# A linear-attention and mixture-of-experts kernel: two v casts moved to ScalarE, a third exp buffer, the first expert products split, and a planner that knows a shared memory port

## The chip, the cores and the metric

The kernel runs on one core of one Trainium2 chip. The metric is the device time in microseconds of one execution. Before the change it was 982.22 us (median of 3 runs, 981.87 to 985.09). The span that a profile shows is about 1.8 us shorter than the time of the same execution.

Engine names: PE is TensorE's matmuls, PEld its weight loads, DVE is VectorE, ACT is ScalarE, POOL is GpSimd, SP is SyncE.

## The reference, cut to what matters

```python
def phi(x):                                     # elu + 1
    return np.where(x > 0, x, np.exp(x) - 1.0) + 1.0
q_p, k_p = phi(q), phi(k)                       # q, k, v: 8 batches, 8 heads, 576 x 64
kv  = np.einsum('bhsd,bhse->bhde', k_p, v)
z   = np.sum(k_p, axis=2)
x   = einsum(q_p, kv) / (einsum(q_p, z) + 1e-6)   # -> 4608 rows of 512
P   = exp(x @ w_gate - max);  8 rounds of row and column normalisation
out = sum over e of P[:, e] * (relu(x @ w1[e]) @ w2[e])    # 8 dense experts, F = 1024
```

The attention is small. The expert products are almost all of the work.

## The kernel before

The attention is done in 16 units, each a batch and half of its heads. A unit loads k, q and v, makes phi of k and q (exp on ACT, min and max on DVE), casts v to 16 bits on GpSimd, and sends them through kv, den, num and two transposes to x transposed (`xT`). The products of expert 0 run beside all this as far as their rows of `xT` are complete. Matmuls of nothing (`warm`) fill PE until then.

The program emits its instructions through a planner. It simulates the engines with estimated times and emits each task when its simulated turn comes. Each engine then runs its own list in that order, on the chip as well:

```python
def add(self, eng, fn, deps=(), prio=0.0, acq=(), use=(), lat=0.0, after=0.0): ...
def slot(t):
    r = t["ready"]
    ...                                    # and when buffers of its pools come free
```

The parts of a unit that the change touches (cut):

```python
def att(b, g):
    n = 2 * b + g
    ...
        (nc.gpsimd if n in (2, 3) else nc.sync).dma_start(...)   # k, q, v of the unit
    ...
    te = fadd(("act", 1.17), f_e, ...)                           # exp
    tph[nm] = fadd(("dve", 1.35), f_m, deps=[te, tt_], ...)      # min, max: phi
    ...
    def f_v(e):
        copy(e, gvv["tile"][:, :, :, 0:D], gin["v"]["tile"])     # the v cast
    tvv.append(fadd(("pool", 1.3), f_v, deps=[ta, tin["v"]], ...))
    vcast[n] = tvv[0]
```

The order of the first weights is set with the cast:

```python
att(0, 0)
att(0, 1)
w_t = {0: load_w1(0, prio=-290.0, parts=2, deps=[vcast[0]])}   # issued on GpSimd's queue
```

`deps` is known to the planner alone. It says that the load is planned after the cast. No data passes from the cast to the load, so no semaphore is made for it. The load waits on the chip only because both stand in GpSimd's one list.

The softmax here doesn't subtract the row's maximum and nothing guards it: scores larger than these inputs give would overflow.

## Time and profile before

| | before |
|---|---|
| time, median of 3 | 982.22 us |
| span of the profiled execution | 982.2 us |
| PE busy | 962.2 us, 98% |
| first kv product of unit 0 starts | 9.12 us |
| denominators of unit 0 reach DVE (`rden`, 1e-6 added, just before the reciprocal) | 14.74 us |
| first product of expert 0 starts | 22.53 us |
| PE idle from 22.5 to 120 us | 8.6 us |

### The profile page before, as it was taken

The numbers are of one execution on the slowest core, as the hardware profiler recorded it, in microseconds if no ns is written. First come the engines' busy times: TensorE is split into PE (matmuls) and PEld (weight loads), VectorE is DVE, ScalarE is ACT, GpSimd is POOL, SyncE is SP. The second block draws the span as 40 slices with busy tenths as digits, with TensorE's granted clock in tenths as the row PEclk, the third lists the DMA queues.
The fourth block names the chain that finished last, engine by engine and source line by source line (L and its number), as shares of the span: only waits on it lengthen the run. The fifth ranks groups of instructions, "written<-read, shape, count | busy, mean of one in ns | idle before, by whom it ended". The sixth has DMA issues, their size and how long they took to land.

```text
span 982.2 us, 21403 instructions
## 1 busy us (share of the span) xinstructions
PE 962.2 (98%) x8716; PEld 792.7 (81%) x8716; DVE 771.7 (79%) x1561; ACT 563.2 (57%) x1034; POOL 127.9 (13%) x171
## 2 busy tenths in 40 slices
PE   7899999999999999999999999999999999999997
PEld 4455564488888888888888888888888888888885
DVE  6898869967777777777777777777777777777774
ACT  4798754565555555555555555555555555555552
POOL 4111200001111111111111111111111111111110
PEclk9999999999999999999999999999999999999999
DMA  9886953162226312272225322272225322236663
GB/s 318 257 303 239 265 160 140 65 127 77 75 76 142 97 73 76 76 161 76 77 75 137 101 76 75 76 162 76 76 76 137 102 76 76 76 103 168 161 161 98
DMA packets 47029, 121.99 MB, mean 124 GB/s; under 512 B 4177, under 2 KB 18001, under 8 KB 46929
## 3 DMA queue, kind: packets, MB, share of 16 engines
q1 hardware_dynamic: 32128, 99.76, 30.3%
q0 software_dynamic: 14480, 20.33, 11.5%
q8 instruction: 68, 1.11, 0.5%
q10 hardware_dynamic: 320, 0.52, 0.1%
q14 instruction: 33, 0.26, 0.1%
HBM read 119.69 MB, written 17.69 MB: 140 GB/s over the span
## 4 chain that ended last, share of the span: by engine, by line
PE 89%; DVE 1%; ACT 1%; issue 0%
PE ye L809 33%; PE hq L627 23%; PE att L627 11%; PE Zye L627 6%; PE Zye L809 6%; PE ye L706 5%; PE hq L536 4%; PE xt_ps L387 0%; PE kv_ps L306 0%; PE num_ps L371 0%; PE lg_ps L405 0%; DVE tk L281 0%; PE qt_ps L332 0%; ACT tq L272 0%; PE den_ps L347 0%; ACT qpT L221 0%
## 5 line engine op out<-in xcount | busy, mean ns | idle before, releaser
L823 DVE SCALAR_TENSOR_TENSOR acc<-ye,P_sb,acc 128x256 f32<-128x256 f32 x620 | 264.9, 477 | 95.3 <-PE ye L809 77.9
L627 PEld LDWEIGHTS <-W 128*128 128x128 f16 x2016 | 197.1, 98 | 23.7
L809 PEld LDWEIGHTS <-S 128*128 128x128 f16 x1984 | 194.1, 98 | 22.7 <-issue 0.3
L809 PE MATMUL ye<-T,S 128*128 128x256 f16 x1488 | 192.8, 273 | 0.1
L833 POOL TENSOR_TENSOR acc<-acc,st 128x256 f32<-128x256 f32 x124 | 87.5, 725 | 625.6 <-ACT st L830 620.7
L653 ACT ACTIVATE h<-hq 128x512 f16<-128x512 f32 x126 | 76.3, 606 | 160.8 <-PE hq L627 160.8
L627 PEld LDWEIGHTS <-w 128*128 128x128 f16 x1512 | 147.6, 98 | 23.3 <-issue 1.0
L809 PEld LDWEIGHTS <-h 128*128 128x128 f16 x1488 | 145.6, 98 | 16.8
L627 PE MATMUL hq<-xs,W 128*128 128x256 f16 x1008 | 151.2, 273 | 0.0
L627 PE MATMUL att<-xs,W 128*128 128x256 f16 x1008 | 151.2, 272 | 0.0
L627 PE MATMUL hq<-xs,w 128*128 128x256 f16 x1008 | 140.7, 272 | 0.8 <-DVE h L656 0.8
L782 DVE TENSOR_TENSOR S<-h 128x1024 f16<-128x1024 f16 x124 | 85.4, 688 | 57.9 <-ACT h L653 57.9
L656 DVE CUSTOM_DVE_ANT_0 h<-att,s 128x512 f16<-128x512 f32 x126 | 86.7, 688 | 13.1 <-ACT s L643 13.1
L830 ACT ACTIVATE st<-Zye,P_sb 128x256 f32<-128x256 f32 x124 | 52.1, 471 | 78.0 <-PE Zye L809 78.0
L643 ACT COPY s<-hq 128x512 f32<-128x512 f32 x126 | 75.0, 595 | 36.7 <-PE hq L627 36.7
L650 ACT ACTIVATE h<-Zye 128x512 f16<-128x512 f32 x126 | 75.2, 597 | 35.1 <-PE Zye L627 35.1
L656 DVE CUSTOM_DVE_ANT_0 h<-hq,s 128x512 f16<-128x512 f32 x126 | 86.5, 686 | 0.8 <-PE hq L627 0.7
L639 ACT COPY Zye<-hq 128x512 f32<-128x512 f32 x126 | 73.3, 581 | 16.3 <-PE hq L627 16.3
L706 PE MATMUL ye<-w,h 128*128 128x512 f16 x320 | 77.6, 379 | 0.9 <-DVE acc L223 0.9
L627 PE MATMUL Zye<-xs,w 128*128 128x256 f16 x504 | 75.6, 273 | 0.0
L647 ACT COPY s<-att 128x512 f32<-128x512 f32 x126 | 74.5, 591 | 0.0
L536 PE MATMUL hq<-xT,w 128*128 128x512 f16 x288 | 70.6, 379 | 2.4 <-ACT h L540 2.2
(90 smaller groups left out, 963.1 us busy)
## 6 DMA issues: line engine op xcount, KB each, us to landing
xs<-xd SPq DMA_DIRECT2D x63, 896.0 KB, 4.6
w<-in_moe_w_dram POOLq DMA_DIRECT2D x14, 1024.0 KB, 11.7
out_dram<-acc SPq DMA_DIRECT2D x68, 128.0 KB, 2.4
kin<-in_k_dram SPq DMA_DIRECT2D x14, 576.0 KB, 6.0
qin<-in_q_dram SPq DMA_DIRECT2D x14, 576.0 KB, 5.0
vin<-in_v_dram SPq DMA_DIRECT2D x14, 576.0 KB, 6.4
xd<-xst SPq DMA_DIRECT2D x9, 512.0 KB, 2.6
xd<-xT SPq DMA_DIRECT2D x9, 256.0 KB, 7.1
```

Source lines behind the costliest of these rows:

```text
L536: nc.tensor.matmul(ghq["tile"], lhsT=gw1["tile"][:, c, ts(f, P)], rhs=xT[:, c, ds(512 * g, 512)], start=(c == 0), stop=(c == NDT - 1))
L627: nc.tensor.matmul(dst[:, p, :], lhsT=lhs(p, c), rhs=rhs(c), start=(first and p == 0 and c == 0), stop=(c == 1), skip_group_check=True)
L643: nc.scalar.copy(out=gs2["tile"], in_=gX["tile"])
L647: nc.scalar.copy(out=gs5["tile"], in_=gR["tile"])
L650: nc.scalar.activation(out=hd(0, 0), in_=Zt[1], func=AF.Relu)
L653: nc.scalar.activation(out=hd(1, 0), in_=gX["tile"], func=AF.Relu)
L656: nc.vector._custom_dve(TENSOR_ADD_SAT, out=dst, in0=ps, in1=sb, s0=3.0e38, s1=0.0)
L706: nc.tensor.matmul(gy[tt]["tile"], lhsT=gh["tile"][:, f, ds(P * tt, P)], rhs=gw2["tile"][:, f, :], start=(f == 0), stop=(f == NFT - 1))
L782: nc.vector.tensor_tensor(out=Sx[:, i], in0=a0, in1=a1, op=op)
L809: nc.tensor.matmul(bank(g_)[:, s, :], lhsT=lhs(s, kk), rhs=rhs(kk), start=(new and s == 0 and kk == 0), stop=(kk == 3), skip_group_check=True)
L823: nc.vector.scalar_tensor_tensor(out=dst(), in0=bank(g_)[:, s, :], scalar=P_sb[:, gg, e:e + 1], in1=dst(), op0=ALU.mult, op1=ALU.add)
L833: nc.gpsimd.tensor_tensor(out=dst(), in0=dst(), in1=gst["tile"], op=ALU.add)
```

## The change

Its intent, in the order of the diff: the planner is told that a v cast on GpSimd locks the memory port that DVE's phi needs; a third buffer for the results of exp; the v casts of units 0 and 1 on ACT, which is idle there; the first two tiles of the first expert product split in halves of the contraction, so that half can run on the `xT` of unit 0 alone.

```diff
     def run(self):
+        locked = [0.0]
         def slot(t):
-            r = t["ready"]
+            r = max(t["ready"], locked[0]) if t["port"] else t["ready"]
 ...
+            if t["lock"] and e == "pool":
+                locked[0] = t["done"]
 ...
-    p_e = S_.pool(2)
+    p_e = S_.pool(3)
 ...
+    VACT = (0, 1)
 ...
-            tph[nm] = fadd(("dve", 1.35), f_m, ..., prio=pr)
+            tph[nm] = fadd(("dve", 1.35), f_m, ..., prio=pr, port=True)
 ...
-        tvv.append(fadd(("pool", 1.3), f_v, ..., prio=pr))
+        tvv.append(fadd(("pool", 1.2) if n not in VACT else ("act", 1.17), f_v, ..., prio=pr, lock=True))
 ...
-        for f in range(NFT):
-            ghq = S_.grp(p_hq)
+        jobs = [(f, 0, NDT) for f in range(NFT)]
+        if g == 0:
+            jobs = [(f, c, c + 2) for c in (0, 2) for f in range(2)] + jobs[2:]
+        for f, c0, c1 in jobs:
 ...
-            t1 = add(("pe", 0.87), f_hq, deps=[tw1[f // 4], prev_hq[0]] + xd_, ...)
+            t1 = add(("pe", 0.2175 * (c1 - c0)), f_hq,
+                     deps=[tw1[f // 4], prev_hq[0]] + xd_[0:c1 if g == 0 else None], ...)
```

(cut: the signatures of `add`, `bufs=3` at the exp tile, and the bookkeeping of the halves.)

More of the change, by code (lines that the diff above doesn't have):

```diff
@@ L31, in grp, with add @@
         return {"pool": pool, "users": [], "tile": None}
-    def add(self, eng, fn, deps=(), prio=0.0, acq=(), use=(), lat=0.0, after=0.0):
+    def add(self, eng, fn, deps=(), prio=0.0, acq=(), use=(), lat=0.0, after=0.0, lock=False, port=False):
         if isinstance(eng, tuple):
@@ L37, in add @@
         k = len(self.t)
-        t = {"eng": eng, "fn": fn, "prio": prio, "acq": tuple(acq), "lat": lat, "kids": [], "nd": 0,
+        t = {"eng": eng, "fn": fn, "prio": prio, "acq": tuple(acq), "lat": lat, "lock": lock, "port": port, "kids": [], "nd": 0,
              "ready": after, "done": None, "id": k}
@@ L264, in f_e @@
             def f_e(_, ge=ge, nm=nm):
-                ge["tile"] = fp.tile([P, 2, NJ, D], FP16, tag="e", name="e" + nm)
+                ge["tile"] = fp.tile([P, 2, NJ, D], FP16, tag="e", name="e" + nm, bufs=3)
                 nc.scalar.activation(out=ge["tile"], in_=gin[nm]["tile"], func=AF.Exp)
@@ L285, in att @@
                        acq=[gt[nm]], use=[gin[nm]], prio=pr)
-            tph[nm] = fadd(("dve", 1.35), f_m, deps=[te, tt_], use=[ge, gt[nm], gin[nm]], prio=pr)
+            tph[nm] = fadd(("dve", 1.35), f_m, deps=[te, tt_], use=[ge, gt[nm], gin[nm]], prio=pr, port=True)
         gvv = S_.grp(p_vv)
@@ L294, in f_v @@
             copy(e, gvv["tile"][:, :, :, 0:D], gin["v"]["tile"])
-        tvv.append(fadd(("pool", 1.3), f_v, deps=[ta, tin["v"]],
-                        use=[gvv, gin["v"]], prio=pr))
+        tvv.append(fadd(("pool", 1.2) if n not in VACT else ("act", 1.17), f_v, deps=[ta, tin["v"]],
+                        use=[gvv, gin["v"]], prio=pr, lock=True))
         vcast[n] = tvv[0]
@@ L529, in layer1, with f_hq @@
         tha = add(("none", 0.0), f_ha, deps=[prev_hq[0]], acq=[gh], prio=g - 400.0)
-        for f in range(NFT):
-            ghq = S_.grp(p_hq)
-            def f_hq(_, f=f, ghq=ghq):
-                ghq["tile"] = hqp.tile([P, 512], FP32, tag="hq", name="hq")
-                for c in range(NDT):
+        ghqs = [S_.grp(p_hq) for f in range(NFT)]
+        jobs = [(f, 0, NDT) for f in range(NFT)]
+        if g == 0:
+            jobs = [(f, c, c + 2) for c in (0, 2) for f in range(2)] + jobs[2:]
+        for f, c0, c1 in jobs:
+            ghq = ghqs[f]
+            def f_hq(_, f=f, ghq=ghq, c0=c0, c1=c1):
+                if c0 == 0:
+                    ghq["tile"] = hqp.tile([P, 512], FP32, tag="hq", name="hq")
+                for c in range(c0, c1):
                     nc.tensor.matmul(ghq["tile"], lhsT=gw1["tile"][:, c, ts(f, P)], rhs=xT[:, c, ds(512 * g, 512)],
@@ L540, in f_rl @@
                 nc.scalar.activation(out=gh["tile"][:, f, :], in_=ghq["tile"], func=AF.Relu)
-            t1 = add(("pe", 0.87), f_hq, deps=[tw1[f // 4], prev_hq[0]] + xd_, acq=[ghq], use=[gw1],
+            t1 = add(("pe", 0.2175 * (c1 - c0)), f_hq, deps=[tw1[f // 4], prev_hq[0]] + xd_[0:c1 if g == 0 else None],
+                     acq=[ghq] if c0 == 0 else [], use=[gw1] + ([ghq] if c0 > 0 else []),
                      prio=g + 0.1 * f + 0.35)
@@ L544, in layer1 @@
             x_users.append(t1)
+            if c1 < NDT:
+                continue
             th.append(add(("act", 0.6), f_rl, deps=[t1, tha], use=[ghq, gh], prio=g - 400.0))
```

## The prediction

> **What bounds the kernel now.** I read the engine totals first, then the table of stretches, then the timeline of the first 40 us.
>
> ```profile
> PE 962.2 (98%) x8716; PEld 792.7 (81%) x8716; DVE 771.7 (79%) x1561; ACT 563.2 (57%) x1034; POOL 127.9 (13%) x171
> PE 89%; DVE 1%; ACT 1%; issue 0%
> ```
>
> The first line is the busy time of each engine, the second the share of each engine in the chain that ended last. TensorE (PE) sets the time. The table of stretches (columns: length, busy us and instructions of PE, PEld, DVE, ACT, POOL, then granted PE clock, DMA share, GB/s) says where it does not:
>
> ```profile
> 9.10:22.50 13.40, 11.48 (x131) 7.03 (x131) 11.71 (x25) 5.90 (x11) 9.17 (x12) 0.87 1.12 325
> 22.50:30.00 7.50, 4.41 (x44) 2.13 (x41) 5.17 (x9) 5.83 (x8) 2.73 (x2) 1.00 1.15 277
> 60.00:80.00 20.00, 17.59 (x174) 10.27 (x172) 19.45 (x36) 19.31 (x31) 3.96 (x4) 1.00 0.88 300
> 140.00:160.00 20.00, 20.00 (x117) 9.97 (x115) 17.79 (x48) 9.16 (x17) 0.00 (x0) 1.00 0.56 215
> 300.00:900.00 600.00, 599.92 (x5465) 534.10 (x5463) 471.74 (x919) 334.51 (x635) 76.34 (x106) 1.00 0.34 96
> ```
>
> From 120 us to 900 us PE is full. The total of matmuls is fixed by the algorithm and the change removes none, so time can only be won where PE waits or runs filler: before 22.5 us, and in the idle gaps from 22.5 to 120 us, which add up to 8.6 us (97.5 us less the PE busy time of those stretches: 3.1, 0.2, 1.4, 2.4, 0.25 and 1.2 us). "Busy" before 22.5 us includes 34 warm-up matmuls that compute nothing. The useful matmuls of the first two attention units are per unit kv 0.69, transposes of q 0.68, den 0.42, num 0.77, transposes of x 0.72 us = 3.3 us, so 6.6 us for both; about 16 of the first 22.5 us are a pure start-up latency. The 6.6 us of PE idle after 900 us is the drain at the end, and the change does not touch it.
>
> What the start-up consists of, from the timeline (start, length, engine, line, operation, count, idle before):
>
> ```profile
> 7.92 1.15 POOL L225 CAST vv<-vin 128x1152 f16<-128x1152 f32 x1 [6.61 <-DMA vin<-in_v_dram]
> 7.94 1.43 DVE L275 TENSOR_SCALAR eq<-eq 128x1152 f16<-128x1152 f16 x1
> 9.41 1.43 DVE L281 SCALAR_TENSOR_TENSOR tq<-qin,eq 128x576 f16<-128x576 f32 x2
> ...
> 12.39 1.15 POOL L225 CAST vv<-vin 128x1152 f16<-128x1152 f32 x1 [0.28 <-DMA vin<-in_v_dram]
> ...
> 12.41 2.40 DVE L281 SCALAR_TENSOR_TENSOR tk<-kin,ek 128x576 f16<-128x576 f32 x2
> ...
> 14.74 0.17 DVE L353 TENSOR_SCALAR rden<-den_ps 128x20 f32<-128x20 f32 x1
> ...
> 22.45 1.18 ACT L221 COPY xT<-xt_ps 128x576 f16<-128x576 f16 x2 [3.05 <-PE xt_ps L387]
> ...
> 22.53 0.99 PE L536 MATMUL hq<-xT,w 128*128 128x512 f16 x3
> ...
> 23.68 1.24 PE L536 MATMUL hq<-xT,w 128*128 128x512 f16 x5 [0.16 <-ACT xT L221]
> ```
>
> DVE's min on eq takes 1.43 us here; the same instruction on ek at 6.10 us took 0.46 us. The pair that makes tk at 12.41 us takes 2.40 us where the pair at 6.60 us took 1.43 us. Both lie beside a GpSimd cast of v. Each costs DVE 0.97 us on the chain input, exp, phi, transpose, den, reciprocal, normalise, x transposed, first expert product. In the whole front I find nine such lengthened instructions, 7.1 us in sum: these two, and seven (5.1 us) between 27 and 113 us.
>
> **What the Trainium skill says.** "SBUF — State Buffer", section "Who interferes with whom": GpSimd's port pair is DVE's second pair, an exclusive lock for a whole instruction; tensor_scalar in a two-port mode, or a DVE instruction with two SBUF inputs against a GpSimd instruction that reads SBUF, blocks or is blocked, and the one that issued first wins. The trace agrees: 1.15 us of cast, 0.97 us of delay, and where DVE was first the cast itself is the long one (1.58 us at 27.25 us against 1.15 us). The same section says ACT has ports of its own, so a cast there should delay nothing. "TensorE: Matmul & The Clock Gate", section "What's actually happening": a clock gate halves PE's clock after a stretch of low activity. The trace agrees: the granted clock is 0.5 from about 11.7 to 15.1 us. "Perfetto Trace Analysis", section "Identifying the Most-Contended Engine", prefers weight-load time and useful work to matmul busy time; I follow it by not counting warm-up as work.
>
> **The change part by part.**
>
> First, the v casts of units 0 and 1 go to ACT, after its exps. vin lands at 7.9 us; ACT ends the exp of q at 7.54 us, so the first cast ends near 9.1 us, as on GpSimd. The cost of 1.16 us (ACT's other f32 to f16 passes over 128x1152 take that) falls where ACT was idle from 7.54 to 9.46 us. DVE's eq then ends at 8.45, tq at 9.93 instead of 10.84 us. Next on DVE come four kvz copies (all four now on DVE, 0.93 us as at 29.35 us) and the shorter qpT copy, to about 11.3 us; min 0.46 and tk 1.43 us uncontended end at 13.1 instead of 14.8 us. So rden, and with it xn and x transposed of unit 0, come 1.7 us earlier. Unit 1: its v cast on ACT comes after exp and add of q, 13.4 to 14.6 us, a us later than on GpSimd, but its kv product sits behind unit 0's x transposes on PE, at 17.44 us before and near 15.75 us now, so that is hidden. Unit 1's x transposed should be complete about 1.7 us earlier, near 21.9 instead of 23.6 us.
>
> Second, the split. In the instruction order of the changed PE, two hq matmuls now stand in unit 1's wait for qpT, where three warm-ups stood, and the two halves of the second tile fill the wait for the last x copy. The kernel before already ran c=0 and 1 of the first tile ahead of that copy, as waits are per instruction (three matmuls at 22.53, the next at 23.68 us). So the split brings two matmuls, 2 x 0.217 = 0.43 us, not four. The first half of w1 was issued at 9.0 us and landed 5.9 us later, at 14.9 us, so the early pair does not stall PE's queue at about 17.3 us.
>
> Third, the third e buffer lets an exp start before the previous phi is finished. At the start it gives nothing: the second exp of k began at 9.46 us and its data lands at 2.26 + 7.1 = 9.4 us.
>
> Fourth, the planner now puts phi after a cast that is planned beside it. This only reorders: 14 casts stay on GpSimd. From 20 us on the orders of PE, ACT and DVE differ nearly everywhere until attention ends, then are the same. In the changed order PE has 160 instead of 136 second-layer matmuls behind it when the last x transpose comes, with 164 first-layer ones in both: 24 x 0.217 = 5.2 us more useful work. Part is a later end of attention (planned phis wait), part less PE waiting. I count 1 us as real: of the 5.1 us of later DVE delays perhaps half goes, and in 40 to 80 us, where DVE and ACT are over 93% busy and PE idles 3.9 us, perhaps 40% of that reaches PE.
>
> Against this stands DMA. Transfers run without a pause from 2 to 40 us at 207 to 408 GB/s, so vin of units 2 and 3 (landed 22.8 and 27.2 us) comes no earlier. PE has ready hq work then, so I take only 0.3 us off.
>
> Sum: 1.7 + 0.43 + 1.0 - 0.3 = 2.8 us; with a little for gaps behind the earlier relus, 3 us. 982.2 - 3.0 = 979.2.
>
> **Rivals.** (a) The inputs absorb the head start: unit 2 and 3 wait for DMA, and all but the 0.4 us of the split and a little hq work is lost, 981.3 us. For it: GpSimd waited 2.95 and 3.15 us for vin there. Against: PE idled 3.1 us in that stretch for ACT's relus (1.4 us) and for tq (1.6 us), not for DMA. (b) The new order fits the chip much better: all of the planned 5.2 us is real on top of the start-up, 975 us. For it: nine delays gone would be 7.1 us of DVE time in its fullest stretch. Against: PE idles only 4 us from 40 to 80 us, and nothing stops a real cast from colliding when real times slip from planned ones. (c) The order fits worse: a static order that takes hq groups ahead of kv makes PE wait in line and exps come late on ACT, giving back 2 to 3 us: 982 to 983 us. For it: ACT has two more passes, 2.3 us. Against: they lie before 15 us, where ACT has slack.
>
> **Range and chances.** (a) and (b) set the ends: 976.3 to 981.4 us. Two per cent is 19.6 us, more than all PE idle and start-up latency that a reorder could reach, so within 2%: 0.985; faster 0.01, slower 0.005.
>
> **What would show it.** Right: no GpSimd cast before 20 us; eq's min 0.46 us and unit 1's tk pair 1.43 us; rden near 13.1 us; first hq matmuls as a pair near 17.5 us; the steady run of hq near 20.8 us; PE full after 120 us as before. Wrong: PE idle between 22.5 and 120 us not below 8 us, DVE delays beside casts still near 5 us, or the half-clock stretch moved onto the first hq products. The prediction fails low if attention's end falls behind and PE runs dry, and high if those gaps vanish.

## More of the kernel before

The prediction shows the main lines. Two more views are needed later. The first is the timeline of GpSimd (start, length, engine, line, operation, count, idle before and its releaser):

```profile
9.00 1.66 POOL L207 DMA_DIRECT2D w<-in_moe_w_dram  x2
10.66 0.72 POOL L253 DMA_DIRECT2D kin<-in_k_dram  x1
...
22.95 1.15 POOL L225 CAST vv<-vin 128x1152 f16<-128x1152 f32 x1 [2.95 <-DMA vin<-in_v_dram]
```

The w1 load follows the first v cast at 9.00 us. The cast of unit 2 waits for its input until 22.95 us.

The second is the DMA view, for the stretch from 7 to 8 us (queue, packets, MB, share of the 16 engines' time) and for the first 13 us (transfer, count, size, median us from issue to landing):

```profile
q1 hardware_dynamic: 183, 0.40, 103.4%
...
vin<-in_v_dram SPq DMA_DIRECT2D x2, 576.0 KB, 7.6
```

Until w1 is issued, the hardware queue with the inputs of units 0 and 1 has the DMA engines to itself and moves 0.40 MB in a microsecond.

One caution on this profile. Its execution took 983.97 us, almost 2 us over the median of the kernel before.

## The result, and the profile after

| | before | after |
|---|---|---|
| median of the same rounds (4 runs each) | 982.29 us (981.87 to 985.09) | 985.08 us (984.15 to 986.27) |
| ratio | | 1.0023, 95% interval 1.0001 to 1.0045 |

A ratio here is the mean time of one kernel's runs over the mean of the other's runs of the same rounds, so it is not quite the ratio of the medians that are quoted. The class is "same", but the time is 2 to 3 us up, where 3 us down was predicted, and it is outside the predicted range.

The engine totals and the chain that ended last hardly differ from before. PE still sets the time:

```profile
PE 962.5 (98%) x8716; PEld 792.9 (81%) x8716; DVE 768.1 (78%) x1560; ACT 567.2 (58%) x1037; POOL 128.9 (13%) x169
PE 92%; DVE 4%; ACT 2%; DMA 2%; issue 1%; SPq 0%; DVEq 0%; ACTq 0%
```

The table of stretches answers to the one in the prediction:

```profile
9.10:22.50 13.40, 9.50 (x110) 5.98 (x110) 8.44 (x22) 7.82 (x10) 5.33 (x8) 0.87 1.10 338
22.50:30.00 7.50, 6.15 (x40) 2.84 (x38) 4.73 (x8) 5.04 (x8) 3.49 (x4) 1.00 1.13 294
60.00:80.00 20.00, 19.05 (x200) 11.52 (x200) 17.43 (x38) 16.68 (x26) 4.11 (x3) 1.00 0.56 189
300.00:900.00 600.00, 599.91 (x5466) 534.21 (x5464) 471.82 (x919) 334.60 (x635) 76.66 (x107) 1.00 0.34 96
```

The middle of the kernel is the same, and 60 to 80 us is fuller than before, 19.05 against 17.59 us. The loss is at the start. The timeline of the first 27 us, with the same instructions as those that the prediction shows of before:

```profile
1.44 1.66 POOL L211 DMA_DIRECT2D w<-in_moe_w_dram  x2
...
8.05 0.46 DVE L281 TENSOR_SCALAR eq<-eq 128x1152 f16<-128x1152 f16 x1
8.54 1.43 DVE L287 SCALAR_TENSOR_TENSOR tq<-qin,eq 128x576 f16<-128x576 f32 x2
...
10.09 1.16 ACT L225 CAST vv<-vin 128x1152 f16<-128x1152 f32 x1 [2.46 <-DMA vin<-in_v_dram]
...
14.72 1.43 DVE L287 SCALAR_TENSOR_TENSOR tk<-kin,ek 128x576 f16<-128x576 f32 x2
...
16.06 0.17 DVE L359 TENSOR_SCALAR rden<-den_ps 128x20 f32<-128x20 f32 x1
...
21.23 0.59 PE L547 MATMUL hq<-xT,w 128*128 128x512 f16 x2
...
25.03 0.99 PE L547 MATMUL hq<-xT,w 128*128 128x512 f16 x3
```

Read from the bottom: the steady run of expert products starts at 25.03 us (22.53 before), `rden` of unit 0 at 16.06 us (14.74 before), the v cast at 10.09 us (7.92 before), because its input came late. The two DVE delays are gone, as planned: min on eq takes 0.46 us and the pair for tk 1.43 us. The first line tells why the input came late. The w1 load went out at 1.44 us, 7.6 us earlier than before.

The DMA view of the same two stretches as before:

```profile
q1 hardware_dynamic: 88, 0.19, 56.2%
q0 software_dynamic: 90, 0.09, 54.9%
...
vin<-in_v_dram SPq DMA_DIRECT2D x2, 576.0 KB, 11.8
w<-in_moe_w_dram POOLq DMA_DIRECT2D x2, 512.0 KB, 14.2
```

From 7 to 8 us the inputs now share the DMA engines with w1, about half of the time each, and move 0.19 MB where they moved 0.40 MB. v takes 11.8 us to land, not 7.6 (median of units 0 and 1). The Trainium skill, "DMA: Bandwidth & Descriptors", section "SWDGE vs HWDGE vs iDMA", says that software-generated and hardware-generated transfers feed different internal queues of each DMA engine and that the engine serves them in turn. The trace agrees: w1 moves almost nothing before 6 us (a share of 4.8% from 5 to 6 us), when k and q of unit 0 have nearly landed, and then both queues move side by side, with shares of 56.2% and 54.9% from 7 to 8 us. The inputs that pay are v of unit 0 and all of unit 1, which were issued after w1.

### The profile page after: what moved, and what is told of

It is laid out like the page before. It is cut to its first block, busy times and chain, and to the rows that moved or that the text cites. A ratio compares the mean times of both kernels' runs of the same rounds, so it can differ in the third digit from the quotient of the medians.

```text
span 982.9 us, 21418 instructions
## 1 busy us (share of the span) xinstructions
PE 962.5 (98%) x8716; PEld 792.9 (81%) x8716; DVE 768.1 (78%) x1560; ACT 567.2 (58%) x1037; POOL 128.9 (13%) x169
## 4 chain that ended last, share of the span: by engine, by line
PE 92%; DVE 4%; ACT 2%; DMA 2%; issue 1%; SPq 0%; DVEq 0%; ACTq 0%
PE ye L823 33%; PE hq L641 23%; PE att L641 11%; PE ye L720 6%; PE Zye L641 6%; PE Zye L823 6%; PE hq L547 5%; DMA vin<-in_v_dram 2%; PE xt_ps L393 1%; PE num_ps L377 1%; PE kv_ps L312 1%; PE qt_ps L338 1%; DVE tk L287 1%; DVE tq L287 1%; DVE xn L382 1%
```

## The experiments

Every kernel below was compared with runs of the kernel before on the same chip in the same rounds. All gave the right result but for two that are wrong, as told there.

A measure used below, called **lead**: in the kernels that keep the plan of the kernel before, PE's list is the same, so the start of the same group of matmuls can be compared between two profiles. The lead is how many us earlier it starts than in the control (e12_before_again); a minus says later.

### Does the early w1 load cost the time?

**e1_gate.** The changed kernel with a tiny copy of one column of the cast v on GpSimd in front of the first w1 load. The load now has to wait as it did before. No order is planned anew.

```diff
+                if e == 0 and nm == "w1" and i == 0:
+                    gt_s = const.tile([P, 1], FP16, tag="gate", name="gate")
+                    nc.gpsimd.tensor_copy(out=gt_s, in_=vv_t[0][:, 0, 0, 0:1])
                 nc.gpsimd.dma_start(out=dst, in_=AP(...))
```

> The changed kernel, with one tiny GpSimd copy (128x1) that reads the first cast v put in front of the first weight load on GpSimd's queue, so that this load waits for the cast on ScalarE as it waited for the cast on GpSimd before. Instruction orders are else unchanged. Theory T (the change set the first weight load free: it is issued at 1.44 us instead of 9.0 us, takes bandwidth from the first q, k and v, and vin lands at 10.1 instead of 7.9 us; all else in the change is a gain): vin lands near 7.9 us, first kv product near 9.1 us, rden of unit 0 near 13.1 us instead of 16.1 us, and the time is 979 to 981 us, 4 to 6 us under the changed kernel and 1 to 3 us under the kernel before. Rival R1 (the new instruction orders from 22 to 120 us cost it): first kv is early too, but the time stays within 1.5 us of 985. Rival R2 (the casts delay ScalarE's exps): 983 to 985 us.

Measured: 982.38 us (981.22 to 983.22), before 981.95; ratio 1.0003 (0.9990 to 1.0016). The changed kernel itself was at 1.0022 in its repeat below. So the early load costs 0.0019 of 982 us, 1.9 us (the two intervals together leave some 1.8 us either way). The start is then nearly as predicted: v cast on ACT at 8.17, `rden` at 13.67, steady expert products at 21.47 us; 0.6 to 0.7 us are missing, with the kv and q transposes of unit 0 at a halved clock (1.02 and 1.14 us). Still nothing is gained on the kernel before. Theory T is half right: the load costs time, but what is left is not a gain of 1 to 3 us.

**e2_early_w1.** The other way round: the kernel before with both w1 loads issued at set-up, every other order kept.

```diff
+        early = e == 0 and nm == "w1"      # tile made and both dma_starts emitted at once;
+            if early: fn(None, now=True)   # the planned task then does nothing
```

> The kernel before, with only the two halves of the first weight load issued ahead of everything on GpSimd's queue; plan and orders of all else unchanged, casts of v on GpSimd, no split. Theory T: vin of unit 0 lands near 10 us instead of 7.9, the first kv product moves to about 11.3 us, and the time rises by 2 to 4 us over the kernel before (984 to 986 us). R1 and R2, which see no harm in the early load: within 1 us of the kernel before.

Measured: 987.20 us (984.97 to 988.87), before 981.95; ratio 1.0051 (1.0038 to 1.0065). The early load alone costs the kernel before 5 us: w1 goes out at 1.24 us, the v casts start at 10.20 and 20.46 us (7.92 and 12.39 before), `rden` of unit 0 at 16.16 us. That is more than the 2 to 4 us that theory T expected.

**e6_after_again.** The changed kernel once more, to have it beside the others.

```diff
 (no edit)
```

> The changed kernel itself once more, on the same chip as the next three runs, so that the cost of the early weight load can be read against them directly. All theories: 984 to 986 us; granted clock 0.995 to 0.997, below the 0.998 to 1.000 of the kernel before.

Measured: 984.94 us (983.34 to 985.76), before 982.17; ratio 1.0022 (1.0010 to 1.0035). The loss is real.

**e7_gate_warm.** e1_gate with eight more warm-ups before the first kv product, so that the half-clock stretch at the start (mean granted clock 0.87 from 9.1 to 22.5 us in the first profiles of both kernels) goes away.

```diff
+        nwarm[0] += 1
-        nc.tensor.matmul(yw[0], ...)
+        for _i in range(9 if nwarm[0] == 16 else 1):
+            nc.tensor.matmul(yw[0], ...)
```

> The changed kernel with the first weight load held back (as e1_gate) and eight more warm-up matmuls before the first kv product, which fill PE's gap from about 7.3 to 9.1 us. Theory H (what e1_gate failed to win of the predicted 3 us is eaten by half-clock stretches at the start: kv and q transposes of unit 0 took 1.02 and 1.14 us instead of 0.69 and 0.68): those two are back at 0.69 and 0.68 us, rden of unit 0 near 12.9 us, mean granted clock 0.999 or more, time 980.5 to 981.7, about 1 us under e1_gate. Rival (a head start at the front is lost downstream whatever its size, in order waits and DMA): first parts as above, time within 0.5 us of e1_gate's 982.4.

Measured: 982.94 us (981.36 to 986.11), before 982.17; ratio 1.0009 (0.9992 to 1.0027). The half clock at the start went (1.00 throughout), and no gain came: theory H fell. Two of the six runs are at 986 us, so this is shown only to about 1.7 us.

### The parts alone, each planned anew

**e3_casts_on_pool.** The changed kernel with all v casts on GpSimd.

```diff
-    VACT = (0, 1)
+    VACT = ()
```

> The changed kernel with all casts of v on GpSimd again (planner, third e buffer and split stay). GpSimd's cast holds the first weight load back again, so T: load issued near 9.0 us, vin at 7.9 us, the two DVE delays of 0.97 us at 7.9 and 12.4 us are back, and the time is 980.5 to 982.5 us, under the changed kernel by 2.5 to 4.5 us. R1 (orders from the planner cost it): 984 us or more. R2: 981 to 983 us as well; it is told from T by e1_gate and by the second run of this set.

Measured: 987.88 us (985.99 to 990.20), before 981.95; ratio 1.0057 (1.0043 to 1.0071). A miss for theory T: without the ACT casts, and with the w1 load nearly in its old place (9.57 us), it is slower still, as rival R1 said of the new orders.

**e5_act_casts_only.** The kernel before with the two casts on ACT alone, planned anew.

```diff
+    VACT = (0, 1)
-        tvv.append(fadd(("pool", 1.3), f_v, ...
+        tvv.append(fadd(("pool", 1.3) if n not in VACT else ("act", 1.17), f_v, ...
```

> The kernel before with only the first two casts of v on ScalarE, no gate, planner and split as before. T: the first weight load is issued near 1.4 us, first kv near 11.3 us, time 984 to 986 us as in the changed kernel: this part alone carries the loss. R1 (the planner's knowledge of the port costs it): within 1 us of the kernel before. R2: 983 to 985 us too, but with vin landing at 7.9 us.

Measured: 988.21 us (987.72 to 989.78), before 981.95; ratio 1.0064 (1.0052 to 1.0076). w1 goes out at 1.43 us as theory T said, but the loss is larger than its 984 to 986 us, so the new order costs something of its own.

**e4_act_casts_gate.** e5 with the gate of e1_gate.

```diff
 (e5_act_casts_only and the gate)
+                    nc.gpsimd.tensor_copy(out=gt_s, in_=vv_t[0][:, 0, 0, 0:1])
```

> The kernel before with only the first two casts of v on ScalarE and the first weight load held back by a tiny GpSimd copy; planner and split as before. It is e5_act_casts_only but for the gate. Theory T: the load near 10 us, vin near 8 us, first kv near 9.4 us, and the time falls by 4 us or more from e5's 988.2, to 981 to 984 us. If e5's loss came from its instruction orders after 40 us (half-clock stretches at 50 and 67 us in its profile), it stays at 986 us or more.

Measured: 990.27 us (989.69 to 990.96), before 982.17; ratio 1.0078 (1.0066 to 1.0091). A clear miss. The gate did not help here. In its trace PE waits 2.9 us for the w2 load between 30 and 40 us, and its clock is halved once near 52 us.

**e8_split_only.** The kernel before with the split of the first expert products.

```diff
+        if g == 0:
+            jobs = [(f, c, c + 2) for c in (0, 2) for f in range(2)] + jobs[2:]
```

> The kernel before with only the split of the first two products by halves of the contraction. By the prediction's count: 0.4 us less, 981.3 to 982 us. Rival S (any edit makes the planner draw a new order after 25 us, and orders differ by several us whatever the edit does itself): 984 us or more, with PE idle or half-clock stretches after 40 us that the kernel before has not.

Measured: 983.90 us (982.15 to 984.33), before 982.17; ratio 1.0011 (0.9998 to 1.0024). No gain, where 0.4 us was expected. The pair ran early, at 18.63 us, as meant.

**e10_port_only.** The kernel before with the planner's knowledge of the port, and the cast's estimate of 1.2 us.

```diff
+            r = max(t["ready"], locked[0]) if t["port"] else t["ready"]
+            if t["lock"] and e == "pool":
+                locked[0] = t["done"]
```

> The kernel before with only the planner's knowledge of the port (lock and port flags, cast at 1.2 instead of 1.3 in the plan); casts on GpSimd, two e buffers, no split. My prediction took 1 us of gain for this part (with the third e buffer): 980.7 to 981.7. Rival S (a new order is a new draw, and most draws are worse than the tuned one): 984 to 988 us, with PE waits or half-clock stretches after 40 us.

Measured: 983.58 us (982.05 to 985.21), before 981.92; ratio 1.0011 (0.9994 to 1.0027). No gain, where about 1 us was expected.

**e11_e3_only** and **e19_e3_again.** The third exp buffer alone, twice.

```diff
-    p_e = S_.pool(2)
+    p_e = S_.pool(3)
-                ge["tile"] = fp.tile([P, 2, NJ, D], FP16, tag="e", name="e" + nm)
+                ge["tile"] = fp.tile([P, 2, NJ, D], FP16, tag="e", name="e" + nm, bufs=3)
```

> The kernel before with only the third e buffer. Prediction: nothing at the start, so 981.5 to 982.5 us. Rival S: a new draw of the order, 983 to 988 us.

Measured: 981.05 us (980.65 to 981.57), before 981.92; ratio 0.9985 (0.9973 to 0.9997). Of all kernels here only this run's interval lies below 1. Because it was picked out of many, it was run again:

> The third e buffer alone once more: it was the only one of the kernels with an interval below 1 (0.9985, 0.9973 to 0.9997), picked out of many, so it could be luck of the run. If the gain is real: 0.998 to 0.999, below 981.3 us. If it was luck of the draw: 0.9995 to 1.0005.

Measured: 981.78 us (981.14 to 982.85), before 982.35; ratio 0.9994 (0.9981 to 1.0008). The two together suggest about 0.001, 1 us. It is the best kernel that was found, and its gain is not settled.

What these six edits teach is that the parts do not add up. An edit that makes the planner run with other times gives another order for all of the attention, and such orders differ by up to 0.8%. The next group therefore keeps the plan.

### The casts alone, with the plan kept

**e12_before_again.** The kernel before, as control.

```diff
 (no edit)
```

> The kernel before itself, for a second profile. Its first profile came from an execution 2 us slower than its median (983.97 against 982.2 us) and shows 8.6 us of PE idle between 22.5 and 120 us. If part of the predicted gain was counted from idle that a usual execution has not, the profile of a usual one (981 to 982.5 us) shows less: 6 to 7.5 us. If the idle is the same 8.6 us, the base of my sum was right and the loss is elsewhere.

Measured: 981.98 us (981.69 to 982.50), before 981.92; ratio 0.9995 (0.9982 to 1.0007). Its profile has 6.5 us of PE idle from 22.5 to 120 us, as expected of a usual execution.

**e13_cast_same_plan.** The planner still believes that the casts are on GpSimd. Only the emitted instruction goes to ACT. The order on PE, DVE and SP is that of before; ACT has two casts more, GpSimd two fewer and the gate.

```diff
-            copy(e, gvv["tile"][:, :, :, 0:D], gin["v"]["tile"])
+            copy("act" if n < 2 else e, gvv["tile"][:, :, :, 0:D], gin["v"]["tile"])
+                    nc.gpsimd.tensor_copy(out=gt_s, in_=vv_t[0][:, 0, 0, 0:1])
```

> The kernel before with its plan and every instruction order kept, only that the first two casts of v are emitted on ScalarE at their planned place instead of GpSimd, and the first weight load is held back by a tiny GpSimd copy of the first cast v. No new order is drawn. This is my prediction's first step alone. If the step is right: eq's min 0.46 us, the second tk pair 1.43 us, rden of unit 0 near 13.3 us (14.7 before), the last copy of unit 1's x near 22 us (23.6), time 980.3 to 981.2 us, 1 to 1.7 us under the kernel before. Rival (the inputs of units 2 and 3, bound by DMA, absorb the head start): first parts as above, time within 0.5 us of the kernel before.

Measured: 982.62 us (982.48 to 982.93), before 981.92; ratio 1.0002 (0.9989 to 1.0014). This tests the first step of the prediction alone, but for the w1 load, which goes out at 10.12 us here. The timeline of e12_before_again:

```profile
14.64 0.17 DVE L353 TENSOR_SCALAR rden<-den_ps 128x20 f32<-128x20 f32 x1
...
22.44 0.99 PE L536 MATMUL hq<-xT,w 128*128 128x512 f16 x3
...
23.52 1.15 POOL L225 CAST vv<-vin 128x1152 f16<-128x1152 f32 x1 [3.13 <-PE hq L536]
```

and of e13_cast_same_plan:

```profile
12.91 0.17 DVE L356 TENSOR_SCALAR rden<-den_ps 128x20 f32<-128x20 f32 x1
...
20.89 0.99 PE L539 MATMUL hq<-xT,w 128*128 128x512 f16 x3
...
24.75 1.27 POOL L228 CAST vv<-vin 128x1152 f16<-128x1152 f32 x1 [2.14 <-DMA vin<-in_v_dram]
...
39.83 1.02 PE L709 MATMUL ye<-w,h 128*128 128x512 f16 x4 [0.76 <-DMA w<-in_moe_w_dram]
```

The head start is there, 14.64 - 12.91 = 1.73 us at `rden` and 1.55 us at the expert products. But the v of unit 2 is cast at 24.75 us, as soon as it lands and 1.23 us later than in the control, and at 39.83 us PE waits for w2. At the x transposes of unit 2 the head start has become a delay (35.62 against 35.40 us).

**e14_gate_vin.** The same with the gate on the loaded v of unit 0 in place of the cast v, so that w1 goes out about as early as before.

```diff
-                    nc.gpsimd.tensor_copy(out=gt_s, in_=vv_t[0][:, 0, 0, 0:1])
+                    nc.gpsimd.tensor_copy(out=gt_s, in_=v0[0]["tile"][:, 0, 0, 0:1])
```

> The earlier run that kept the whole plan of the kernel before and only put two v casts on ACT had its gate on the first cast v, so the first w1 load started after that cast, and w2 landed at 34.2 and 39.8 us. Here the gate reads the loaded v of unit 0 instead, so w1 should start about as early as in the kernel before (near 9 us). If the late w1/w2 and the inputs of units 2 and 3 behind them are what ate the 1.7 us head start, w2 lands before 34 us, PE has no wait for it, and the time is about 0.7 to 1.2 us below the earlier run's ratio of 1.0002: ratio 0.9985 to 0.9995. If instruction order or the arrival of units 2 and 3 alone decides, the ratio stays at 1.000 to 1.001.

Measured: 982.49 us (981.57 to 983.07), before 981.81; ratio 1.0002 (0.9987 to 1.0016). A miss on the time. The wait for w2 is gone, and v of unit 2 is there at 22.71 us. The lead at the kv products of unit 1 is 1.72 us, and it is lost all the same. The profile shows three DVE instructions lengthened beside a GpSimd cast:

```profile
22.71 1.15 POOL L228 CAST vv<-vin 128x1152 f16<-128x1152 f32 x1 [2.55 <-DMA vin<-in_v_dram]
...
22.91 1.27 DVE L281 TENSOR_SCALAR ek<-ek 128x1152 f16<-128x1152 f16 x1 [2.60 <-ACT ek L272]
...
42.62 1.39 POOL L228 CAST vv<-vin 128x1152 f16<-128x1152 f32 x1 [3.29 <-DMA vin<-in_v_dram]
...
43.11 1.51 DVE L284 TENSOR_TENSOR tq<-tq,eq 128x1152 f16<-128x1152 f16 x1
...
47.95 2.37 DVE L287 SCALAR_TENSOR_TENSOR tq<-qin,eq 128x576 f16<-128x576 f32 x2
...
48.49 1.22 POOL L228 CAST vv<-vin 128x1152 f16<-128x1152 f32 x1 [4.48 <-DMA vin<-in_v_dram]
```

In the control the same three take 0.46, 0.76 and 1.43 us. They are longer here by 0.81, 0.75 and 0.94 us, and the lead falls across them from 1.72 to 0.92, from 0.88 to 0.45 and from 0.45 to -0.49 us (kv products of units 1, 3, 4, 5 and 6). The earlier times have made new collisions on the port: phi starts earlier than in the control, and the three casts start when their v lands.

### Are the inputs the reason?

**e17_before_light** and **e18_cast_light.** The kernel before and e13_cast_same_plan, both with the k, q and v loads of units 2 and 3 cut to a quarter. The rest of their tiles holds data of units 0 and 1, so both give a wrong result, with a relative error of 0.38. All instructions and orders stay.

```diff
+                gr["tile"] = kept[(n - 2, nm)] if n in (2, 3) else fp.tile(...)
+                ... [:, :, 0:144 if n in (2, 3) else NJ * D]      # of 576 columns
```

> Wrong results on purpose: the kernel before with the k, q and v loads of units 2 and 3 cut to a quarter (stale data of units 0 and 1 in the rest), all orders kept. Takes some 7 us of traffic from the 2 to 40 us stretch. If input arrival binds the kernel before itself in 20 to 40 us, it gains some tenths of a us (981.0 to 981.8); if it doesn't, it is the same (981.9).

> The same cut loads with the two v casts on ACT, the plan of the kernel before and the gate on the cast v. If it is the arrival of units 2 and 3 and w2 that absorbs the 1.7 us head start, this is 1.0 to 1.7 us faster than the light kernel before of this call. If the head start is lost in the order of instructions or in PE's later work, the two light kernels are within 0.4 us of one another.

Measured: e17 982.66 us (981.80 to 983.62), ratio 1.0004 (0.9991 to 1.0017); e18 981.21 us (980.48 to 982.41), ratio 0.9994 (0.9980 to 1.0008); before 981.81. With the loads light, the casts on ACT win 1.45 us between the medians and 1.2 us between the means (the spread of the five runs each leaves 0.1 to 2.3 us). With full loads they lost 0.6 us (e13 against e12, medians, not clear of noise). They were run at other times. So no suffering of the kernel before from the loads of units 2 and 3 is shown, and the kernel with the head start does suffer from them; the evidence is just clear of noise. The timeline of e18_cast_light:

```profile
12.78 0.17 DVE L361 TENSOR_SCALAR rden<-den_ps 128x20 f32<-128x20 f32 x1
...
22.11 1.15 POOL L228 CAST vv<-vin 128x1152 f16<-128x1152 f32 x1 [0.61 <-DMA vin<-in_v_dram]
...
41.97 0.72 PE L395 MATMUL xt_ps<-ident,xn 128*128 128x128 f16 x10
```

The cast at 22.11 us is already that of unit 3 (29.15 us in e13). The transposes at 41.97 us come 1.53 us before the control's 43.50 and 2.52 us before e13's 44.49: with the inputs there, the head start lasts.

The lead at the start of the kv products of a unit, in us, from the profiled executions:

| unit | 0 | 1 | 2 | 3 | 4 | 5 | 6 | 15 |
|---|---|---|---|---|---|---|---|---|
| e12, control: starts at | 9.68 | 17.34 | 27.15 | 32.59 | 44.16 | 48.68 | 55.13 | 122.77 |
| e13, casts on ACT | 0.30 | 1.72 | 1.08 | 0.31 | -0.98 | -0.84 | -0.64 | -0.75 |
| e14, gate on the loaded v | 0.22 | 1.72 | 1.45 | 0.92 | 0.88 | 0.45 | -0.49 | -0.61 |
| e18, casts on ACT, light loads | 0.41 | 1.85 | 1.69 | 1.53 | 1.53 | 1.79 | 1.87 | 1.39 |

The spans of these profiles differ from the control's by about as much as the last column says (-0.9, -0.8 and 1.2 us). e18 has none of the three collisions of e14 (min on ek at 22.94 us is 0.17 us longer, the other two are as usual). So the light loads take away both the waits for inputs and the collisions, and these runs don't say how much each is worth.

### Combinations

**e15_e3_gate_vin.** The third exp buffer with its plan, the casts emitted on ACT and the gate on the loaded v.

```diff
 (e11_e3_only, and)
+            copy("act" if n < 2 else e, gvv["tile"][:, :, :, 0:D], gin["v"]["tile"])
+                    nc.gpsimd.tensor_copy(out=gt_s, in_=v0[0]["tile"][:, 0, 0, 0:1])
```

> The third e buffer alone (0.9985) with its own plan, the two casts on ACT and the same gate on the loaded v. If the two gains add: 0.997 to 0.998, near 979.5 us. If the head start is taken by the input loads whatever the rest: 0.9985, 980.5 to 981 us. If it is worse than 0.9985 the casts on ACT cost something later.

Measured: 981.65 us (979.91 to 981.88), before 981.81; ratio 0.9990 (0.9977 to 1.0003). The casts on ACT add nothing to the buffer.

**e16_after_gate_vin.** The changed kernel with the gate on the loaded v.

```diff
+                    nc.gpsimd.tensor_copy(out=gt_s, in_=v0[0]["tile"][:, 0, 0, 0:1])
```

> The changed kernel with its first w1 load held back only until the v of unit 0 has landed (as early as in the kernel before), in place of the gate on the cast v that gave 1.0003. If the early w1 was the whole loss of the changed kernel and the arrival of inputs takes the rest of its head start: 0.9995 to 1.0005. If the late w1 and w2 of the first gate cost something of their own: 0.998 to 0.9995.

Measured: 981.72 us (980.09 to 982.17), before 982.35; ratio 0.9990 (0.9977 to 1.0002). Its timeline:

```profile
8.31 1.67 POOL L214 DMA_DIRECT2D w<-in_moe_w_dram  x2
...
13.23 0.17 DVE L365 TENSOR_SCALAR rden<-den_ps 128x20 f32<-128x20 f32 x1
...
17.31 0.59 PE L553 MATMUL hq<-xT,w 128*128 128x512 f16 x2
...
21.04 0.99 PE L553 MATMUL hq<-xT,w 128*128 128x512 f16 x3
...
23.64 1.15 POOL L232 CAST vv<-vin 128x1152 f16<-128x1152 f32 x1 [3.29 <-DMA vin<-in_v_dram]
```

One copy of 128 elements, with no other edit and no new plan, takes the changed kernel from 1.0022 to 0.9990, 3.1 us (here too some 1.8 us either way). That is the price of the moved load in the changed kernel, 1.9 to 3.1 us with e1_gate. The two gates are not told apart: their intervals overlap. The start is now what was predicted, to 0.25 us. Yet about 1 us is gained on the kernel before, not 3, and its interval still holds 1.

## Why the prediction was wrong

It fails at the first step, in what that step took as given, and then in the deduction for DMA.

**The first step, its mechanism.** Right. No GpSimd cast runs before 20 us, min on eq takes 0.46 us, unit 1's tk pair 1.43 us. Where the w1 load is held (e13), `rden` is 1.73 us earlier; 1.7 was predicted. Where the changed kernel gets its gate back (e16), the predicted marks "rden near 13.1", "a pair near 17.5" and "the steady run near 20.8" are measured at 13.23, 17.31 and 21.04 us.

**The first step, what it took as given.** Wrong. It said "vin lands at 7.9 us", and in the second step "The first half of w1 was issued at 9.0 us and landed 5.9 us later", and carried both over to the changed kernel. But the cast was what kept w1 at 9.0 us, by standing in front of it in GpSimd's list. With the cast on ACT nothing on the chip stood in front, and w1 went out at 1.44 us. v of unit 0 landed at 10.1 us and `rden` came at 16.06 us, 1.3 us later than before in place of 1.7 us earlier. (Of the way there, 0.9 us is a halved clock: kv and q transposes of unit 0 took 1.16 and 1.14 us, 0.69 and 0.68 before.) This was to be seen before any run: no semaphore stands before that load in the changed instruction order. I had read that order for PE, ACT and DVE, and not for the DMA issues of GpSimd.

**The deduction for DMA.** The term was 0.3 us and it is mis-sized. With the plan kept and w1 held, all of the 1.7 us is lost, by 35 us in e13 and by 56 us in e14 (both 1.0002), and 1.2 to 1.45 us come back when the loads of units 2 and 3 are cut (e18 against e17). This is rival (a) in its outcome. Its mechanism, a wait for inputs, is seen in e13, where v of unit 2 and then w2 come late (beside two collisions, of 0.96 and 0.82 us). In e14 these waits are gone, and the lead goes in three new port collisions. The prediction names that danger against rival (b) ("nothing stops a real cast from colliding") and gave it no term. The argument against it was "PE idled 3.1 us in that stretch for ACT's relus and for tq ... not for DMA". That was true of the kernel before, and e17 agrees with it, as lighter loads show no gain there. It does not carry over to a kernel that is 1.7 us earlier while its inputs are not. The Trainium skill, "DMA: Bandwidth & Descriptors", section "Issuing engines are not separate DMA queues", says that transfers of all issuers run on the same 16 engines and interleave. The trace agrees: the inputs of units 2 and 3 and w2 (GpSimd) and those of units 4 on (SyncE) keep the DMA engines busy almost without a pause from 4 to 35 us, whoever issued them (DMA share 1.04 to 1.13 in e13).

**The second step.** 0.43 us was expected, 1.0011 (0.9998 to 1.0024) measured. The pair runs early, at 18.63 us, and nothing follows from it. My reading, not tested: work that PE does early here is taken from what it would do a little later in its waits for the attention.

**The third step.** Expected nothing; 0.9985 and 0.9994 measured. It may be worth 1 us. The prediction looked only at the start, where it holds, and not at the later units. What it does there was not tested.

**The fourth step.** 1.0 us was called real. It fell: 1.0011 alone. The prediction's 24 matmuls, 5.2 us, are there: where all four steps stand and w1 is held (e16), 160 second-layer matmuls lie before the last x transpose, 136 in the control, and 164 first-layer ones in both. But that transpose comes at 140.00 us, 134.45 in the control, 5.55 us later, so all of it is a later end of attention and none is a shorter wait. The lengthened DVE instructions from 20 to 120 us make 5.1 and 3.0 us in sum in two profiles of the kernel before, 4.5 and 4.4 us in two of the changed kernel, and 6.9 us in e16: they vary between executions of one kernel, and no fall is shown. (The prediction counts seven from 27 to 113 us; I find six there, with the same sum.) Nor are they PE's time. From 40 to 60 us PE is busy 17.48 us, where before it was 18.55 (19.24 in the control), and from 60 to 120 us 58.23, where it was 56.12 (56.66). The new order moves PE's waits from one stretch into the other. And the profile that the 8.6 us of idle were read from was of an execution nearly 2 us above its median; the control has 6.5 us, and the changed kernel 6.6. The prediction's sign of failure, "idle not below 8 us", was drawn from an unusual execution.

**The rivals.** (a) is what became of the head start: with the load held (e16) the time is 981.72 us, and (a) had said 981.3. (b) fell; its 975 us also lay below the range whose end it was to set, 976.3. (c), 982 to 983 us by a worse order, is near in number, but the gate shows that the order of compute is not what lost the 2.3 us.

In sum, from the ratios: the changed kernel is 2.2 to 2.3 us above before. Of this, 1.9 to 3.1 us is the early w1. That it costs time is clear of noise (e16, e2); how much it costs in the changed kernel is known only to some 1.8 us. What remains of the four steps without it is 1.0 us of gain at best (e16) and none at worst (e1_gate), in place of 3.0.

**What stays open.** The same two casts on ACT with the same gate cost 1.0002 in the old order (e13) and 1.0078 in a newly planned one (e4), 7.5 us by the order alone. Its trace shows a wait of 2.9 us for w2 and a halved clock near 52 us, but I made no experiment on either. For the same reason it is not known why the changed kernel without the ACT casts (e3) is 3.4 us slower than with them.

## What to carry to other kernels

When an instruction moves to another engine, look at what stood behind it in the old engine's list: an order that nobody waits for by semaphore goes with it, and a DMA issue among it can do harm, as it takes bandwidth from what is needed first (here w1, at 1.44 in place of 9.00 us). A head start at the beginning can be lost where the inputs of the following work don't come earlier too, by waits for them or by meeting an engine that still keeps their time; cutting those loads on purpose, with the orders kept, shows whether they matter. Where a planner orders everything, test a part of a change with the plan held, or the new order drowns it (e13 and e4, the same edit, lie 7.5 us apart). To compare two kernels with one order, compare the start of the same instruction.

## What the Trainium skill lacked or had wrong

- "DMA: Bandwidth & Descriptors", section "SWDGE vs HWDGE vs iDMA", has the taking of turns between software and hardware queues, and the runs agree, but not what it costs the transfers beside it. Here inputs fell from 0.40 MB to 0.19 MB in a microsecond, and v landed after 11.8 in place of 7.6 us (median of units 0 and 1), because a weight load on the other queue ran beside them (984.94 against 981.72 us with it held back, in separate rounds).
- The same page has no rate for a load that casts. The w1 load alone moved 205 GB/s in the kernel before (13 to 15 us) at a full DMA share, against 403 GB/s for plain inputs (7 to 8 us). The profile lists half of w1 as 512 KB, which is its size in 16 bits; it is 1 MB in 32 bits in memory. So the count is of bytes that land, and a casting load may cost its source bytes (an estimate from these numbers: 2 x 205 = 410 GB/s read). Its smaller packets, 1.0 KB against 2.2 KB, would be another reason; neither was tested.
- "SBUF — State Buffer", section "Who interferes with whom", has the shared port right, but no size for this pair of operations: a GpSimd cast of 128x1152 beside DVE's min, max or multiply-add lengthened these by 0.75 to 0.98 us, and by less where they overlapped only in part (0.54 us at 65.28 us in the kernel before). A copy of 128x1 on GpSimd took from 0.19 us (e16) to 0.79 us (e13).
- No page tells that an order on an engine's list that no semaphore backs is lost when one of the two instructions moves to another engine. Here it was worth 1.9 to 3.1 us.
